# Gated attention mix on one core: each product of weights and values split over the two halves of the array's rows

## The chip, the cores and the metric

The kernel runs on one core of one Trainium2 chip. Its engines are TensorE (PE in the profile, with PEld for its weight loads), VectorE (DVE), ScalarE (ACT), GpSimd (POOL) and SyncE (SP, which here issues DMAs). TensorE writes its results to PSUM, which has eight banks of 128 partitions by 512 fp32 numbers. The metric is the device time of one execution in microseconds (us), median of several runs.

## The reference

Two attention blocks, A and B, work on the same input x, with weights of their own. Both have 32 heads of 20 features, 2048 tokens and a model width of 640. A gate per token mixes their outputs.

```python
def _A_ref(x, wqkv, wo):                 # _B_ref is the same
    B, S, D = x.shape                    # 1, 2048, 640
    H = 32; Dh = D // H                  # 32 heads of 20
    qkv = (x @ wqkv).reshape(B, S, 3, H, Dh).transpose(2, 0, 3, 1, 4)
    q, k, v = qkv[0], qkv[1], qkv[2]
    p = softmax(einsum("bhqd,bhkd->bhqk", q, k) * Dh ** -0.5, axis=-1)
    o = einsum("bhqk,bhkd->bhqd", p, v)
    return o.transpose(0, 2, 1, 3).reshape(B, S, D) @ wo

g = sigmoid((x * gate_w).sum(-1, keepdims=True))
return g * _A_ref(x, A_wqkv, A_wo) + (1 - g) * _B_ref(x, B_wqkv, B_wo)
```

## The kernel before

**Units and steps.** The 64 heads of A and B are taken in 16 groups of four (GH = 4), and the 2048 queries in four blocks of 512 (QB). One group with one block of queries is a unit; there are 64. A unit's 2048 keys are taken in eight steps of two tiles of 128 keys. So the main loop, over G, has 16 x 4 x 8 = 512 steps.

**What a step does on TensorE.**
- *Scores* (`scores`, L644): for each of the two key tiles and four heads one product with 64 rows, keys against queries, 128 x 512, in a bank of its own. Even heads lie in rows 0 to 63 of the array, odd ones in rows 64 to 127. ScalarE takes the exponential from the bank into an SBUF tile `pt` of 128 keys by 512 queries, fp32 (L647).
- *Maxima* (`max_mm`, L581): the softmax needs each query's largest score before its exponentials are made. It is found up to 15 steps ahead, by products of 60 rows, queries against 512 keys, one in either half of the rows. VectorE reduces most of these banks (L592). Where two chunks of keys are taken together, ScalarE makes a ReLU of a difference (L585), and VectorE combines it with the other bank (L589).
- *Values* (`values`, L662): for each key tile of the step before, one block of four products, one for each head: the stationary operand is 128 keys by 21 columns of V (20 features and a column of ones, which gives the softmax's sum), fp32; the moving operand is `pt`. The four heads write the partitions 0, 32, 64 and 96 on of one bank, `acc`, and are summed there over all 16 key tiles of the unit.
- *Blocks of other work* (L382): projections of later groups (q, k and v from x, as products of fp16 halves) and output projections, up to 15 full-width products into one bank, one block at place 3 of a step's eight places (and at place 6 when it is behind). They are emptied by L409, L537, L727 and L729. Small products are L605, L768, L167 and L184.

**Order.** Everything is issued in an order written out in the loop at the end of the kernel. The eight places q of a step each have one score product and one or two products for maxima; the two blocks of values stand at places 0 and 5 (VPOS), other blocks at places 3 and 6. Each engine takes its instructions in that order.

**Banks.** Seven of the eight banks rotate (`banks`, NB = 7); the eighth is `acc`. `take` chooses, while the program is made, the bank that a small planner expects to be free first. The planner keeps a clock for TensorE, ScalarE and VectorE with estimated costs (`tick_score`, `tick_block`, `spend`, `give`); at run time only the semaphores decide, and a product waits until its own bank was emptied.

**End of a unit.** After the unit's last values, `take_acc` copies `acc` to the SBUF tile `ot` on ScalarE (L747), and the next unit's first values, which overwrite the bank, wait for that copy. The rest is spread over later steps: the sums are inverted, multiplied in (L770) and split into fp16 halves on GpSimd, and SyncE stores them. `take_last` (L788) does this for the last unit without a detour.

**Start.** x is transposed by TensorE (`turn`, L859) into rotating banks; the first six transposed blocks are kept in banks until the scale of x is known, and are then drained by ScalarE and VectorE (L863, L864).

Of the kernel before, what the change touches and what calls it, by code (L numbers as in the profile page):

```python
# [11 lines left out]
F32 = mybir.dt.float32  # L12
I32 = mybir.dt.int32
AF = mybir.ActivationFunctionType
OP = mybir.AluOpType
# [4 lines left out]
P = 128  # L20
# [4 lines left out]
NT = S // P  # L25
NC = D // P
GH = 4
NG = H // GH
GF = GH * DH
QB = 512  # L30
# [4 lines left out]
VW = DH + 1  # L35
# [9 lines left out]
RAMP = 1.5  # L45
BETWEEN = 1.3
VSTART = 14
NB = 7

T_SCORE, T_MODE, T_VALUES, T_READY = 0.217, 0.1, 0.85, 0.39  # L50
T_EXP, T_MAX, T_BACK = 0.478, 0.6, 0.15
# [8 lines left out]
def kernel(  # L60
# [10 lines left out]
    nc = tc.nc  # L71
# [7 lines left out]
    psum = ctx.enter_context(tc.tile_pool(name="psum", bufs=1, space=PSUM))  # L79
# [18 lines left out]
    V = [consts.tile([P, NT, 2 * GH, VW], F32, name=f"v{i}") for i in range(2)]  # L98
    sums = consts.tile([P, P], F32, name="sums")
    nc.gpsimd.tensor_copy(sums.rearrange("p (h e) -> p h e", e=32),  # L100
                          ident.rearrange("p (h e) -> p h e", e=32)[:, :, DH:VW].to_broadcast([P, GH, 32]))
    acc = psum.tile([P, QB], F32, name="acc")
    banks = [psum.tile([P, QB], F32, name=f"bank{i}") for i in range(NB)]
    gates = consts.tile([P, 2, NT], F32, name="gates")
    inv_x = consts.tile([P, 1], F32, name="inv_x")
# [14 lines left out]
    block_end = [0.0, None]  # L120
    free_at, held = [0.0] * NB, set()
    now = [-1]

    def take():

        i = min((k for k in range(NB) if k not in held), key=lambda k: free_at[k])
        held.add(i)
        return i, banks[i]

    def spend(engine, cost, ready=0.0):  # L130

        clock[engine] = max(clock[engine], ready) + cost
        return clock[engine] + T_BACK

    def give(i, t):
        free_at[i] = t
        held.discard(i)
# [7 lines left out]
    def tick_block(cost, ready=0.0):  # L145

        begin = block_end[0] if now[0] < 0 and block_end[1] == rows_free else max(rows_free) + T_MODE
        clock["pe"] = max(begin, ready)
        rows_free[:] = [clock["pe"] + cost + T_MODE] * 2
        block_end[:] = [clock["pe"] + cost, list(rows_free)]  # L150
        clock["done"] = clock["pe"] + cost + T_READY - T_MODE
# [60 lines left out]
    def scales_qk(i, maxima):  # L212

        return scales(maxima, 2, lambda r, inv: set_qk(i, r, inv))
# [171 lines left out]
    def turns(n):  # L386

        for _ in range(n if now[0] >= 0 else 0):
            yield
# [30 lines left out]
    def run(gen):  # L420
        for _ in gen:
            pass
# [35 lines left out]
    def half_tiles(g):  # L458
        blk["q", g] = wts.tile([P, 2, 1024], F16, name="cq", tag="cq", bufs=2)
        return blk["q", g]  # L460
# [93 lines left out]
    def unit_of(u):  # L554
        gq, i = divmod(u, NS)
        g, qb = divmod(gq, NQ)
        return g, qb, i
# [3 lines left out]
    def max_parts(g, qb):  # L561
        m = mparts[g, qb] = wts.tile([P, 2, 2, 4, 4], F32, name="mpart", tag="mpart", bufs=2)
        nc.gpsimd.memset(m[:, :, 0:1 if g else 2, :, 0] if g or qb else m, LOW)
# [62 lines left out]
    ptiles, weighed = {}, {}  # L626
# [30 lines left out]
    def values(G, kk):  # L657
        g, qb, i = unit_of(G)
        tick_block(T_VALUES, weighed.pop((G, kk)))
        kt = 2 * i + kk  # L660
        for h in range(GH):
            nc.tensor.matmul(acc[32 * h:32 * h + VW, :], V[(g // 2) % 2][:, kt, (g % 2) * GH + h, :],  # L662
                             ptiles.pop((G, kk, h)), start=(kt == 0), stop=(kt == NT - 1))


    wo_parts = {}
# [76 lines left out]

    def take_acc(g, qb):

        ot = work.tile([P, QB], F32, name="ot", bufs=2)
        nc.scalar.activation(ot, acc, AF.Copy)  # L747
        spend("act", T_EXP)
        few, many = (2, 8) if g == 2 * NG - 1 else (6, 24)
        sq = work.tile([P, 16], F32, name="sq", bufs=2)  # L750
        sh = work.tile([P, 2, 16], F16, name="sh", bufs=2)
        yield from turns(few)
        nc.sync.dma_start(sq, ot.rearrange("(h e) q -> h e q", e=32)[:, DH, :])
        yield from turns(many)
        nc.vector.reciprocal(sq, sq)
        spend("dve", 0.25)
        nc.gpsimd.tensor_scalar(sq, sq, RS, None, op0=OP.mult)
        nc.gpsimd.tensor_copy(sh[:, 0], sq)
        nc.gpsimd.tensor_tensor(sh[:, 1], sq, sh[:, 0], op=OP.subtract)
        yield from turns(few)  # L760
        sr = work.tile([2 * GH, QB], F16, name="sr", bufs=1)
        for k in range(2):
            nc.sync.dma_start(sr[GH * k:GH * k + GH], sh[:, k])
        yield from turns(many)
        yield PRODUCT
        i, pt = take()
        tick_block(T_SCORE, free_at[i])
        nc.tensor.matmul(pt, sel.rearrange("k h e -> k (h e)"), sr, start=True, stop=True)  # L768
        yield
        nc.vector.tensor_tensor(ot, ot, pt, op=OP.mult)  # L770
        give(i, spend("dve", 0.7, clock["done"]))
        o = work.tile([P, 2, QB], F16, name="on", bufs=2)
        nc.gpsimd.tensor_copy(o[:, 0], ot)  # L773
        nc.gpsimd.tensor_tensor(o[:, 1], ot, o[:, 0], op=OP.subtract)
        if g < 2 * NG - 1:
            yield from turns(16)
            for h in range(GH):
                f = (g % NG * GH + h) * DH
                nc.sync.dma_start(o_scr[g // NG][:, f:f + DH, qb * QB:(qb + 1) * QB].rearrange("k d q -> d k q"),
                                  o[32 * h:32 * h + DH])  # L780
            stored.add((g, qb))
        else:
            last.append((qb, o))

    def take_last():

        ot = work.tile([P, QB], F32, name="ot", bufs=2)
        nc.scalar.activation(ot, acc, AF.Copy)  # L788
        i, pt = take()
        nc.tensor.matmul(pt, sums, ot, start=True, stop=True)  # L790
        rc = work.tile([P, QB], F32, name="fs")
        o = work.tile([P, 2, QB], F16, name="on", bufs=2)
        for t in range(4):
            c = slice(t * P, (t + 1) * P)
            nc.vector.reciprocal(rc[:, c], pt[:, c])
            nc.vector.tensor_tensor(ot[:, c], ot[:, c], rc[:, c], op=OP.mult)
            nc.scalar.activation(o[:, 0, c], ot[:, c], AF.Copy)
            nc.gpsimd.tensor_tensor(o[:, 1, c], ot[:, c], o[:, 0, c], op=OP.subtract)
        give(i, spend("dve", 4.0, spend("act", T_EXP)))
        return o  # L800
# [19 lines left out]
            nc.sync.dma_start(out_t[:, 4 * qb + t, :], y)  # L820


    nc.vector.memset(acc, 0.0)
    start_stack = ExitStack()
    start = start_stack.enter_context(tc.tile_pool(name="start", bufs=1))
    xs = start.tile([P, NT, D], F32, name="xs")
# [26 lines left out]
    def turn(j0, c):  # L853

        n = slice(j0 * P, (j0 + 4) * P)
        i, pt = take()
        for u in range(4):
            tick_block(0.11, free_at[i])
            nc.tensor.transpose(pt[:, u * P:(u + 1) * P], xs[:, j0 + u, c * P:(c + 1) * P], ident)  # L859

        def drain():
            give(i, spend("dve", T_MAX, spend("act", T_EXP, clock["done"])))
            nc.scalar.activation(xh[:, c, n], pt, AF.Copy, scale=r_x)  # L863
            nc.vector.scalar_tensor_tensor(xl[:, c, n], pt, r_x, xh[:, c, n], op0=OP.mult, op1=OP.subtract)  # L864

        return drain

    def turns_of(j0, cs=range(NC)):
        for c in cs:
            turn(j0, c)()  # L870
            yield

    max_parts(0, 0)
    drains = [turn(0, c) for c in range(NC)] + [turn(4, 0)]
    found = []
    run(scales(wm, 5, lambda r, inv: found.extend((r, inv))))
    r, inv = found
# [4 lines left out]
    for f in drains:  # L882
# [7 lines left out]
                            op=OP.subtract)  # L890
# [4 lines left out]
    def a_chunk(ch):  # L895
        if ch % 2 == 0:
            halves.append(half_tiles(0))
        n = slice((ch % 2) * QB, (ch % 2 + 1) * QB)
        hl = halves[ch // 2][:, :, n]
        yield from project_chunk(blk["a", 0], hl[:, 0], hl[:, 1], ch)  # L900
        for pair in range(2):
            run(spread(0, hl, ch * QB, QB, q=(0,) if ch == pair == 0 else (), k=(pair,), queues=both))
# [7 lines left out]
    def beside(gen, n, other):  # L910

        for k, _ in enumerate(gen):
            if k % n == n - 1:
                next(other, None)
        run(other)
# [6 lines left out]
        key_differences(0, halves[half], start.tile([P, QB], F32, name="fd"), start.tile([P, 2, QB], F16, name="dd0"))  # L922
        run(spread_differences(0, both, to))

    beside(a_chunk(0), 2, turns_of(4, range(1, NC)))
    beside(a_chunk(1), 3, turns_of(8))
    differences_of(0, KD[0])
    beside(a_chunk(2), 3, turns_of(12))
# [29 lines left out]
    work = ctx.enter_context(tc.tile_pool(name="work", bufs=2))  # L958
# [22 lines left out]
    for g in range(2 * NG):  # L981
        b = g * NQ * NS
        n = g + 1
        if n < 2 * NG:
# [3 lines left out]
            i = g // 4 + 1  # L988
            if i < 4:
                if g % 4 == 0:  # L990
                    z, c0 = i // 2, 320 * (i % 2)
                    parts = max_tasks([[(wqkv[z], part * D + c0 + 160 * k) for k in range(2)] for part in range(2)],
                                      lambda m, i=i: scales_qk(i, m))
# [98 lines left out]
    for G in range(STEPS + 1):  # L1092
        g, qb, i = unit_of(G)
# [8 lines left out]
        for q in range(8):  # L1102
# [22 lines left out]
            if q == 3:  # L1125
                for f in todo.pop(G, []):
                    f()
                out_tasks(G)
    end_o = take_last()
    while side or parked or fill or current or outs or last:  # L1130
        advance()
# [32 lines left out]
```

## Time and profile before

| | |
|---|---|
| median of three runs | 2894.9 us (2893.07 to 2895.11) |
| the profiled execution's own time | 2894.15 us |
| its span, first to last instruction | 2892.3 us |
| mean granted TensorE clock | 0.995 of full speed |
| TensorE busy (PE) | 2816.3 us, 97% |
| ScalarE busy (ACT) | 2552.8 us, 88% |
| VectorE busy (DVE) | 2431.3 us, 84% |
| GpSimd busy (POOL) | 672.8 us, 23% |

A row of the timeline has the start in us from the span's begin, the duration, engine, line, operation, output and inputs, their shapes, and how many records were merged; in brackets stands how long the engine was idle before it, and what ended that. For a product, `128*21` is the rows and columns of the array that it uses. A row of the groups has the busy time, the mean duration of one in ns, and the idle time before with what ended it. A row of the windows has the stretch, its length, and then for PE, PEld, DVE, ACT and POOL the busy us with the number of instructions, followed by the granted clock, the DMA share and GB/s. A record of a product covers its way through the array too, so records of products that follow each other overlap, and the distance between starts tells more than the duration. An fp32 product is two records.

### The profile page before, as it was taken

The numbers are of one execution on the slowest core, as the hardware profiler recorded it, in microseconds if no ns is written. First come the engines' busy times: TensorE is split into PE (matmuls) and PEld (weight loads), VectorE is DVE, ScalarE is ACT, GpSimd is POOL, SyncE is SP. The second block draws the span as 40 slices with busy tenths as digits, with TensorE's granted clock in tenths as the row PEclk, the third lists the DMA queues.
The fourth block names the chain that finished last, engine by engine and source line by source line (L and its number), as shares of the span: only waits on it lengthen the run. The fifth ranks groups of instructions, "written<-read, shape, count | busy, mean of one in ns | idle before, by whom it ended". The sixth has DMA issues, their size and how long they took to land.

```text
span 2892.3 us, 63590 instructions
## 1 busy us (share of the span) xinstructions
PE 2816.3 (97%) x23474; PEld 979.8 (34%) x23474; DVE 2431.3 (84%) x4643; ACT 2552.8 (88%) x5249; POOL 672.8 (23%) x1096
## 2 busy tenths in 40 slices
PE   6899999999999999999999999999999999999998
PEld 3433223342233323343233333334333333332222
DVE  6688898878898898978988888887788888889973
ACT  3799999989999999988989999998899999888986
POOL 5212112121221212233331111212113243120010
PEclk9999999999999999999999999999999999999999
DMA  4110101001020101102022020111102112122122
GB/s 128 36 45 7 36 11 40 16 12 33 13 53 17 31 15 28 46 13 52 17 47 50 13 59 16 44 39 24 44 21 52 44 39 69 52 67 72 54 61 71
DMA packets 176765, 114.80 MB, mean 40 GB/s; under 512 B 111812, under 2 KB 150396, under 8 KB 176452
## 3 DMA queue, kind: packets, MB, share of 16 engines
q1 hardware_dynamic: 174196, 109.77, 15.8%
q8 instruction: 184, 3.01, 0.4%
q0 software_dynamic: 1600, 0.96, 0.2%
q14 instruction: 129, 1.06, 0.1%
q10 hardware_dynamic: 656, 0.00, 0.0%
HBM read 48.89 MB, written 26.61 MB: 26 GB/s over the span
## 4 chain that ended last, share of the span: by engine, by line
PE 90%; DVE 4%; ACT 2%; DMA 1%; POOL 1%; issue 1%; SPq 0%; DVEq 0%; ACTq 0%; POOLq 0%
PE acc L662 33%; PE bank L644 23%; PE bank L382 19%; PE bank L581 12%; DVE mpart L592 3%; ACT pt L647 2%; PE bank L768 1%; DMA xs<-in_A_x_dram 0%; PE bank L605 0%; PE bank L815 0%; ACT rl L585 0%; DVE mneg L599 0%; DMA wv<-in_A_wqkv_dram 0%; PE bank L184 0%; PE bank L859 0%
## 5 line engine op out<-in xcount | busy, mean ns | idle before, releaser
L647 ACT ACTIVATE pt<-bank 128x512 f32<-128x512 f32 x4096 | 2223.0, 612 | 222.8 <-PE bank L581 194.3
L592 DVE TENSOR_REDUCE mpart<-bank 128x1 f32<-128x512 f32 x2976 | 1912.2, 684 | 342.0 <-PE bank L581 271.1
L644 PE MATMUL bank<-qt,kt 64*128 64x512 f16 x4096 | 1164.8, 381 | 11.6 <-ACT pt L647 7.2
L662 PE MATMUL acc<-pt,v 128*21 128x512 f32 x8192 | 1081.9, 600 | 0.5
L581 PE MATMUL bank<-kt,qt 60*128 60x512 f16 x3536 | 1050.3, 380 | 4.7 <-ACT pt L647 0.7
L644 PEld LDWEIGHTS <-kt 64*128 64x128 f16 x4096 | 281.0, 94 | 1092.7 <-issue 914.6
L589 DVE CUSTOM_DVE_ANT_0 rl<-bank,rl 128x512 f32<-128x512 f32 x560 | 378.6, 681 | 16.2 <-PE bank L581 7.0
L585 ACT ACTIVATE rl<-bank 128x512 f32<-128x512 f32 x560 | 329.4, 594 | 7.9 <-PE bank L581 7.9
L581 PEld LDWEIGHTS <-qt 60*128 60x128 f16 x4096 | 270.8, 94 | 67.3 <-issue 53.9
L382 PE MATMUL bank<-xx,wbh 128*128 128x168 f16 (+2 forms) x2240 | 283.3, 244 | 9.8 <-ACT pt L647 4.3
L662 PEld LDWEIGHTS acc<-pt,v 128*21 128x21 f32 x8192 | 142.9, 99 | 399.1 <-issue 361.7
L773 POOL CAST on<-ot 128x512 f16<-128x512 f32 x63 | 38.5, 611 | 928.4 <-DVE ot L770 891.8
L382 PE MATMUL bank<-xx,wbl 128*128 128x168 f16 (+2 forms) x1120 | 253.4, 243 | 0.0
L382 PEld LDWEIGHTS <-wbh 128*128 128x128 f16 x2240 | 184.5, 98 | 99.9 <-issue 89.8
L581 PE MATMUL bank<-kd,qt 60*128 60x512 f16 x560 | 208.1, 387 | 1.8 <-DMA kd<-dd 1.2
L382 PE MATMUL bank<-woh,o_in 128*128 128x160 f16 (+1 forms) x960 | 156.7, 256 | 4.8 <-ACT pt L647 2.8
L382 PE MATMUL bank<-wvh,xx 128*128 128x160 f16 (+1 forms) x1280 | 155.4, 233 | 5.9 <-ACT pt L647 3.7
L382 PEld LDWEIGHTS <-xx 128*128 128x128 f16 x1920 | 133.5, 97 | 57.8 <-issue 52.5
L382 PE MATMUL bank<-wvl,xx 128*128 128x160 f16 (+1 forms) x640 | 137.3, 231 | 0.6 <-POOL wvl L322 0.6
L382 PEld LDWEIGHTS <-o_in 128*128 128x128 f16 (+1 forms) x1440 | 105.6, 97 | 73.9 <-issue 60.4
L411 POOL CAST cq<-fs 128x512 f16<-128x512 f32 x60 | 36.7, 611 | 364.8 <-ACT fs L409 364.8
L382 PE MATMUL bank<-wol,o_in 128*128 128x160 f16 (+1 forms) x480 | 115.7, 254 | 0.0
(132 smaller groups left out, 1347.3 us busy)
## 6 DMA issues: line engine op xcount, KB each, us to landing
y_scr<-y_out SPq DMA_DIRECT2D x32, 320.0 KB
kt<-cq SPq DMA_DIRECT2D x120, 80.0 KB
o_scr<-on SPq DMA_DIRECT2D x240, 40.0 KB
kt<-cq SPq DMA_DIRECT2D x136, 40.0 KB
xs<-in_A_x_dram SPq DMA_DIRECT2D x8, 640.0 KB
o_in<-o_scr SPq DMA_DIRECT2D x32, 160.0 KB
y_out<-y_scr SPq DMA_DIRECT2D x16, 320.0 KB
xx<-y_scr SPq DMA_DIRECT2D x16, 320.0 KB
```

The lines of the kernel that those rows point to most:

```text
L382: nc.tensor.matmul(out_ap, a, b, start=(k == 0), stop=(k == len(pairs) - 1))
L411: nc.gpsimd.tensor_copy(hi, f)
L581: nc.tensor.matmul(pt, QT[g % 2][r, pair, q0:q0 + P], k, start=True, stop=True)
L585: nc.scalar.activation(relus[u, j], pt, AF.Relu)
L589: nc.vector.tensor_tensor_reduce(rl, pt, rl, 1.0, LOW, OP.add, OP.max, m)
L592: nc.vector.tensor_reduce(m, pt, axis=AX.X, op=OP.max)
L644: nc.tensor.matmul(et, KT[g % 2][r, pair, kt * P:(kt + 1) * P], QT[g % 2][r, pair, qb * QB:(qb + 1) * QB], start=True, stop=True)
L647: nc.scalar.activation(pt, et, AF.Exp, scale=factor(g // 4))
L662: nc.tensor.matmul(acc[32 * h:32 * h + VW, :], V[(g // 2) % 2][:, kt, (g % 2) * GH + h, :], ptiles.pop((G, kk, h)), start=(kt == 0), stop= ...
L768: nc.tensor.matmul(pt, sel.rearrange("k h e -> k (h e)"), sr, start=True, stop=True)
L773: nc.gpsimd.tensor_copy(o[:, 0], ot)
```

## The change

Each product of a head's weights and values over 128 keys becomes two over 64 keys: keys 0 to 63 in rows 0 to 63 of the array, keys 64 to 127 in rows 64 to 127. The two halves are summed in a bank each, `acc0` and `acc1`. At the end of a unit (`sum_acc`), ScalarE copies the first bank to `ot` as before, and VectorE adds the second bank to it. With two banks for sums, six are left to rotate (NB = 6). At the start, five transposed blocks are held in banks ahead of the scales, and the sixth moves behind them to the others of its row of tiles.

```diff
-NB = 7
+NB = 6
...
-    acc = psum.tile([P, QB], F32, name="acc")
+    acc = [psum.tile([P, QB], F32, name=f"acc{i}") for i in range(2)]
...
         for h in range(GH):
-            nc.tensor.matmul(acc[32 * h:32 * h + VW, :], V[(g // 2) % 2][:, kt, (g % 2) * GH + h, :],
-                             ptiles.pop((G, kk, h)), start=(kt == 0), stop=(kt == NT - 1))
+            pt = ptiles.pop((G, kk, h))
+            for half in range(2):
+                r = slice(64 * half, 64 * half + 64)
+                nc.tensor.matmul(acc[half][32 * h:32 * h + VW, :], V[(g // 2) % 2][r, kt, (g % 2) * GH + h, :], pt[r],
+                                 start=(kt == 0), stop=(kt == NT - 1))
+
+    def sum_acc():
+
+        ot = work.tile([P, QB], F32, name="ot", bufs=2)
+        nc.scalar.activation(ot, acc[0], AF.Copy)
+        spend("act", T_EXP)
+        nc.vector.tensor_tensor(ot, ot, acc[1], op=OP.add)
+        spend("dve", T_MAX)
+        return ot
...
     def take_acc(g, qb):
 
-        ot = work.tile([P, QB], F32, name="ot", bufs=2)
-        nc.scalar.activation(ot, acc, AF.Copy)
-        spend("act", T_EXP)
+        ot = sum_acc()
...
     def take_last():
 
-        ot = work.tile([P, QB], F32, name="ot", bufs=2)
-        nc.scalar.activation(ot, acc, AF.Copy)
+        ot = sum_acc()
...
-    nc.vector.memset(acc, 0.0)
+    for t in acc:
+        nc.vector.memset(t, 0.0)
...
-    drains = [turn(0, c) for c in range(NC)] + [turn(4, 0)]
+    drains = [turn(0, c) for c in range(NC)]
...
-    beside(a_chunk(0), 2, turns_of(4, range(1, NC)))
+    beside(a_chunk(0), 2, turns_of(4))
```

## The prediction

> **What bounds the kernel now.** I read the page from the top: the engines' shares, the clock, then the chain that ended last.
>
> ```profile
> span 2892.3 us, 63590 instructions
> PE 2816.3 (97%) x23474; PEld 979.8 (34%) x23474; DVE 2431.3 (84%) x4643; ACT 2552.8 (88%) x5249; POOL 672.8 (23%) x1096
> PEclk9999999999999999999999999999999999999999
> PE acc L662 33%; PE bank L644 23%; PE bank L382 19%; PE bank L581 12%; DVE mpart L592 3%; ACT pt L647 2%; PE bank L768 1%; DMA xs<-in_A_x_dram 0%; PE bank L605 0%; PE bank L815 0%; ACT rl L585 0%; DVE mneg L599 0%; DMA wv<-in_A_wqkv_dram 0%; PE bank L184 0%; PE bank L859 0%
> ```
>
> TensorE is the bound at full clock, and the line that the change rewrites, L662, is a third of the chain. But ScalarE and VectorE, which empty the banks, are not far behind. Since an average hides stages, I next took a stretch from the middle:
>
> ```profile
> 1500.00:2000.00 500.00, 495.87 (x4418) 183.30 (x4417) 422.67 (x801) 451.13 (x937) 103.70 (x177) 1.00 0.16 36
> ```
>
> Columns: PE, PEld, DVE, ACT, POOL. PE 99%, ACT 90%, DVE 85%: three engines almost in balance, joined by seven banks. A program that takes a bank away has to be read for its waits, not only for PE's work. So the last view is the timeline of PE over part of one step:
>
> ```profile
> 1509.10 0.59 PE L644 MATMUL bank<-qt,kt 64*128 64x512 f16 x2
> 1509.32 0.38 PE L581 MATMUL bank<-kt,qt 60*128 60x512 f16 x1
> 1509.62 1.06 PE L662 MATMUL acc<-pt,v 128*21 128x512 f32 x8
> 1510.61 0.39 PE L644 MATMUL bank<-qt,kt 64*128 64x512 f16 x1
> 1510.62 0.39 PE L581 MATMUL bank<-kd,qt 60*128 60x512 f16 x1
> 1510.84 0.38 PE L581 MATMUL bank<-kt,qt 60*128 60x512 f16 x1
> 1510.84 0.59 PE L644 MATMUL bank<-qt,kt 64*128 64x512 f16 x2
> 1511.06 0.38 PE L581 MATMUL bank<-kt,qt 60*128 60x512 f16 x1
> 1511.37 0.24 PE L382 MATMUL bank<-woh,o_in 128*128 128x160 f16 x1
> ```
>
> The pattern: six score and maximum products in pairs, one in each half of the rows, a pair every 0.22 us (1510.62, 1510.84, 1511.06); a block of values (L662); six more; a projection block (L382). A last pair started at 1509.32 streams until 1509.54, and values start at 1509.62: a gap of 0.08. They take 0.99 us to the next score at 1510.61.
>
> **Values, part by part.** A block is four products, each as two passes (eight records). Cutting the timeline inside the block shows its first four passes alone:
>
> ```profile
> 1509.62 0.63 PE L662 MATMUL acc<-pt,v 128*21 128x512 f32 x4
> L662 PE MATMUL acc<-pt,v 128*21 128x512 f32 x8192 | 1081.9, 600 | 0.5
> ```
>
> Four records of about 0.60 end within 0.63, so they start some 0.007 us apart and run side by side in four column groups; the second four start 1.06 - 0.63 = 0.43 to 0.44 us later. 8192 records of eight are 1024 blocks. Of 0.99, two passes are 0.88, the stagger 0.02, and 0.09 is left before the score.
>
> After the change a block is sixteen passes on eight tiles, 64 rows by 32 columns. The halves hold disjoint rows and write different banks, as the pairs of scores already do, so I let all eight run together. The array time stays two passes; the stagger grows by four starts: 4 x 0.007 = 0.027, x 1024 = **+28 us**. Bounds: 0 if each second half starts with its first, as in a score pair (1510.61 and 1510.62), and +911 us if the halves run after each other (two more passes, 0.89 x 1024; a rival below). I take 28, since its row is of this very product.
>
> The Trainium skill prices packed tiles at about 4 ns for each further tile (TensorE: Matmul & The Clock Gate, Part 3, "Measured speedup vs the span model"). By that, an estimate, four more tiles cost 16 ns a block and 17 us in all; the 7 ns above is measured here and decides.
>
> **The gaps at the mode switch** are what a split into halves could save: scores use 64 rows, values 128. If that difference alone drains the array, both gaps of about 0.09 would go. These rows speak on it:
>
> ```profile
> 600.43 0.28 PE L605 MATMUL bank<-ident,mneg 128*16 128x128 f32 x1
> 600.63 1.05 PE L662 MATMUL acc<-pt,v 128*21 128x512 f32 x8
> 89.43 0.31 PE L382 MATMUL bank<-wvh,xx 128*128 128x161 f16 x2
> 89.57 0.27 PE L605 MATMUL bank<-ident,mneg 128*16 128x128 f32 x1
> 89.68 0.23 PE L382 MATMUL bank<-wvl,xx 128*128 128x161 f16 x1
> 2871.50 0.30 PE L815 MATMUL bank<-wbl,on 128*128 128x320 f16 x1
> 2871.63 0.30 PE L815 MATMUL bank<-wbh,on 128*128 128x320 f16 x1
> 2871.86 1.06 PE L662 MATMUL acc<-pt,v 128*21 128x512 f32 x8
> ```
>
> The transpose L605 fits between two full-width products with no gap (0.11 to the next start), so it runs in their mode: 128 rows, full columns. From it to values, only the columns change, and they start 0.20 after it, 0.09 more. L815's products follow each other after 0.13, and values follow L815 after 0.23, again 0.10 more. A change of columns alone costs the same gap. Scores use 128 columns and the new values 32, so I keep both gaps: **0 us**, bounds -184 us (0.18 x 1024) and 0.
>
> Eight more weight loads and eight more products a block must also be issued. The densest stretch:
>
> ```profile
> 86.50:91.50 5.00, 5.00 (x72) 4.97 (x71) 1.68 (x7) 2.91 (x11) 1.29 (x4) 1.00 0.00 0
> ```
>
> 143 instructions in 5 us, 35 ns each. The stretch 1500 to 2000 has 4418 + 4417 = 8835 PE instructions. The program has 512 steps, so some 512/2892 x 500 = 89 in this stretch, with two blocks of values each and 16 more instructions a block: 8835 + 89 x 32 = 11,680, or 43 ns each. Above 35: issue hides behind the streams, **0**.
>
> **Six banks instead of seven.** This is the costly part. Beside the group at 1510.61 stand
>
> ```profile
> 1510.26 0.60 ACT L647 ACTIVATE pt<-bank 128x512 f32<-128x512 f32 x1
> 1511.10 0.60 ACT L647 ACTIVATE pt<-bank 128x512 f32<-128x512 f32 x1 [0.24 <-PE bank L581]
> 1509.93 2.65 DVE L592 TENSOR_REDUCE mpart<-bank 128x1 f32<-128x512 f32 x4
> ```
>
> When the group starts at 1510.61, ScalarE holds one bank until 1510.86, and VectorE, whose four reductions end every 0.66 (1510.6, 1511.2, 1511.9, 1512.6), holds the one that ends at 1511.2. The group takes six: 2 + 6 - 1 = 7 at 1511.06. With six banks the last product waits for 1511.2. Then the L382 block, which began at 1511.37, needs a bank too, and the next to come free is that of the exponential of 1511.10, at 1511.70: 0.33 late, and a signal more, so 0.35. That the delay isn't made up later I read from ScalarE's 0.24 of waiting for PE: its backlog is used up within each step, so it moves along. With 4 products ahead of a block of values nothing waits, and values take no bank. How many such blocks there are is told by what empties them:
>
> ```profile
> L409 ACT ACTIVATE fs<-bank 128x168 f32<-128x168 f32 (+1 forms) x216 | 72.8, 337 | 24.2 <-PE bank L382 23.7 <-POOL on L773 0.5
> L537 ACT ACTIVATE v<-bank 128x160 f32<-128x160 f32 x128 | 42.5, 332 | 6.2 <-PE bank L382 5.6
> L727 ACT ACTIVATE y_out<-bank,f_o 128x160 f32<-128x160 f32 x64 | 26.7, 417 | 1.7 <-PE bank L382 1.6
> L729 DVE SCALAR_TENSOR_TENSOR y_out<-bank,f_o,y_out 128x320 f32<-128x320 f32 x32 | 17.6, 551 | 8.8 <-PE bank L382 5.4 <-ACT pt L647 3.0
> L729 DVE SCALAR_TENSOR_TENSOR xx<-bank,f_o,xx 128x320 f32<-128x320 f32 x32 | 17.5, 550 | 28.9 <-PE bank L382 27.4 <-PE bank L581 0.7 <-PE bank L644 0.6
> ```
>
> 216 + 128 + 64 + 32 + 32 = 472 blocks x 0.35 = **+165 us**. Bounds: 0 if the consumers' slack (10% of ACT) takes it up, and (472 + 512) x 0.35 = +344 if one group before values in each of the 512 steps waits as long.
>
> **Taking the sums.** At the end of a unit the accumulator is copied, and now the second is added on VectorE:
>
> ```profile
> 976.52 0.38 PE L581 MATMUL bank<-kt,qt 60*128 60x512 f16 x1
> 976.86 1.06 PE L662 MATMUL acc<-pt,v 128*21 128x512 f32 x8
> 976.21 0.60 ACT L747 ACTIVATE ot<-acc 128x512 f32<-128x512 f32 x1 [0.19 <-PE acc L662]
> 976.53 0.69 DVE L592 TENSOR_REDUCE mpart<-bank 128x1 f32<-128x512 f32 x1
> L770 DVE TENSOR_TENSOR ot<-ot,bank 128x512 f32<-128x512 f32 x63 | 43.0, 682 | 0.0
> ```
>
> The copy ends at 976.81, and the next values, which overwrite the accumulator, start at 976.86, where the last score pair lets them anyway. The add has the form of L770, 0.68, starts after the copy at 976.87 and ends at 977.55; only then may values begin, on all of PE's queue, 0.7 to 0.75 late. The add stands in VectorE's queue ahead of the reduction of 976.53, so that one and its bank are late too, but PE stands still meanwhile. 63 x 0.75 = **+47 us**; bounds 0 (if values were held by banks there anyway) and 63 x 1.44 = 91 (VectorE has one more reduction of 0.69 ahead). The last unit's add and the four transposes that move behind the scales add **+1**. The add's 43 us of VectorE work lie in its 16% of idle time. The second memset lies beside the loads.
>
> **Sum.** Against the profiled execution's own time, 2894.15 (0.75 below the median of 2894.9, so no correction): 28 + 0 + 165 + 47 + 1 = 241, which is 3135. I forecast **3130 us**, since a few of the stops fall together.
>
> **Rivals.**
> (1) *The bank waits are absorbed.* For: ACT and DVE idle 10 and 15%. Against: ScalarE already waits for PE in the step shown. 2894 + 28 + 48 = 2970.
> (2) *Twice the bank waits*, at values as well: 2894 + 28 + 344 + 48 = 3314. For: seven banks are all in use at 1511.06; against: in the group at 1509.10 six suffice.
> (3) *The halves don't run together*, so the change doesn't do what it says: + 911 + 47; bank waits vanish behind the longer blocks: 3850. Against: scores' halves do, and column groups do; no row shows both at once.
> (4) *Faster*: the row mode is what drains, and both gaps at values vanish: 2894 - 184 + 28 + 48 = 2786 with no bank wait. It decides only while a block's wait is under (184 - 76)/472 = 0.23 us; at 0.35 the time is 2951, slower still. For: no row shows 64 rows going from 128 to 32 columns. Against: L605 and L815 above.
>
> The Trainium skill stands against (4): a change of tiling mode, not of tile, drains the array (TensorEngine Tiling (Array Packing), "Key Properties"). By that rule (4) has no gain left and ends at 3135 or 2970.
>
> **Chances.** Forecast 57%; (1) 18%; (2) 6%; (3) 8%; (4) with its gaps gone 11%, of which 6% on the faster side and 5% near 2951. About 0.2% is what a measurement can tell from no change. Faster 0.06, same 0.02 (the edge of (4)), slower 0.92. The range takes in the forecast, (1) and the slower half of (4), and leaves out (3), the fast half of (4) and the top of (2): 2945 to 3270.
>
> **What would show it.** In L662's rows: sixteen passes within about 1.09 us; two starts at +0.43, not at +0.9. The gap to the next score still 0.09. PE's idle time before L382 and L581, now small, shows ScalarE and VectorE as releasers with some 165 us, and the shares of ACT and DVE fall to about 82 and 79%. Before the first values of a unit, PE waits about 0.7 for the add. I am wrong if L662's block is shorter than now, if PE shows no more bank waits, or if block time doubles.

## The result and the profile after

The changed kernel takes 3134.16 us (median of four runs, 3130.92 to 3135.13), against 2893.99 for the kernel before on the same chips: a ratio of 1.0829 (95% interval 1.0812 to 1.0846), **240 us slower**. 3130 was forecast.

First the page of the changed kernel: its span, the engines, the chain; then the window 1500 to 2000, and two rows of the groups (L665 is the line of the values now).

```profile
span 3133.3 us, 79158 instructions
PE 2980.5 (95%) x31666; PEld 1032.1 (33%) x31666; DVE 2486.8 (79%) x4708; ACT 2602.3 (83%) x5249; POOL 672.0 (21%) x1096
PE acc L665 30%; PE bank L382 18%; PE bank L644 18%; PE bank L581 11%; ACT pt L647 10%; DVE mpart L592 4%; ACT ot L671 1%; PE bank L778 1%; DMA xs<-in_A_x_dram 0%; PE bank L605 0%; DVE mneg L599 0%; PE bank L824 0%; ACT rl L585 0%; DMA wv<-in_A_wqkv_dram 0%; PE bank L184 0%
1500.00:2000.00 500.00, 482.41 (x5293) 166.72 (x5285) 408.58 (x767) 430.35 (x873) 102.95 (x170) 1.00 0.14 32
L665 PE MATMUL acc<-pt,v 64*21 64x512 f32 x16384 | 1107.2, 597 | 0.0
L581 PE MATMUL bank<-kt,qt 60*128 60x512 f16 x3536 | 1121.7, 379 | 62.9 <-ACT pt L647 52.7 <-DVE mpart L592 1.5
```

ScalarE and VectorE fall to 83 and 79% (forecast: 82 and 79), and the exponential L647 rises from 2% to 10% of the chain: PE now waits for what empties its banks. But the idle time of PE in front of L581 is only 63 us. The rest of the wait doesn't look idle: PE's busy time grew by 164 us (2816.3 to 2980.5), though its own work hardly grew. A record of a score lasts 0.38 us, and the next pair is due 0.22 after it, so a start that comes up to 0.16 late leaves no idle time between the records. So starts have to be read. The timeline of PE over one stretch that answers to the one shown of before, with the first passes of its block cut out (second row), and then ScalarE and VectorE beside it:

```profile
1641.06 1.08 PE L665 MATMUL acc<-pt,v 64*21 64x512 f32 x16
1641.06 0.65 PE L665 MATMUL acc<-pt,v 64*21 64x512 f32 x8
1642.08 0.39 PE L644 MATMUL bank<-qt,kt 64*128 64x512 f16 x1
1642.08 0.39 PE L581 MATMUL bank<-kd,qt 60*128 60x512 f16 x1
1642.30 0.38 PE L581 MATMUL bank<-kt,qt 60*128 60x512 f16 x1
1642.31 0.59 PE L644 MATMUL bank<-qt,kt 64*128 64x512 f16 x2
1642.71 0.37 PE L581 MATMUL bank<-kt,qt 60*128 60x512 f16 x1
1643.15 0.23 PE L382 MATMUL bank<-woh,o_in 128*128 128x160 f16 x1
```
```profile
1641.37 1.28 DVE L592 TENSOR_REDUCE mpart<-bank 128x1 f32<-128x512 f32 x2
1642.50 0.60 ACT L647 ACTIVATE pt<-bank 128x512 f32<-128x512 f32 x1 [0.19 <-PE bank L581]
1642.99 0.59 ACT L585 ACTIVATE rl<-bank 128x512 f32<-128x512 f32 x1
```

The block of values is sixteen passes of 0.60: eight start within 0.05 (0.65 - 0.60), the others 0.43 to 0.44 later, and the next score starts 1.02 after the first, 0.03 more than before. The halves do run together. Then five products go as ever, but the sixth, which would start at 1642.52 beside the second of the two L644, waits until 1642.71 for the reduction that gives its bank back (the second of two, over at 1641.37 + 1.28 = 1642.65). The projection block waits for the exponential of 1642.50, which ends at 1643.10, and starts at 1643.15. From the first of the six to the block it is 1.07 us; in the rows of before it was 0.76 (1510.61 to 1511.37).

This can be summed over the whole trace. A stretch is the time from the first score or maximum product after a stop to the next stop (values, block or small product), by the starts of products; sums in us. One block of the trace after, whose next score itself came 0.86 late, is counted in the last row.

| stretch (count) | before | after |
|---|---|---|
| values, first pass to next score (1022 before, 1021 after) | 1011.3 | 1034.3 |
| six products, then a block (389) | 324.8 | 449.5 |
| six products, then values (430) | 332.1 | 376.5 |
| ten products, then values or a small product (95) | 185.0 | 224.4 |
| all else of the span | 1039.1 | 1048.6 |

Of some 240 us, 23 lie in the values themselves, 125 ahead of blocks, 44 ahead of values, 39 in steps without a block, and 10 elsewhere. The 44 lie at one place: the 55 stretches ahead of a unit's first values take 90.0 us against 45.3, and the other 375 take 286.5 against 286.9.

### The profile page after: what moved, and what is told of

Same layout as the page of the kernel before. It is cut to its first block, busy times and chain, and to the rows that moved or that the text cites. A ratio compares the mean times of both kernels' runs of the same rounds, so it can differ in the third digit from the quotient of the medians.

```text
span 3133.3 us, 79158 instructions
## 1 busy us (share of the span) xinstructions
PE 2980.5 (95%) x31666; PEld 1032.1 (33%) x31666; DVE 2486.8 (79%) x4708; ACT 2602.3 (83%) x5249; POOL 672.0 (21%) x1096
## 4 chain that ended last, share of the span: by engine, by line
PE 80%; ACT 11%; DVE 4%; issue 2%; DMA 1%; POOL 1%; SPq 0%; DVEq 0%; ACTq 0%; POOLq 0%
PE acc L665 30%; PE bank L382 18%; PE bank L644 18%; PE bank L581 11%; ACT pt L647 10%; DVE mpart L592 4%; ACT ot L671 1%; PE bank L778 1%; DMA xs<-in_A_x_dram 0%; PE bank L605 0%; DVE mneg L599 0%; PE bank L824 0%; ACT rl L585 0%; DMA wv<-in_A_wqkv_dram 0%; PE bank L184 0%
## 5 line engine op out<-in xcount | busy, mean ns | idle before, releaser
L647 ACT ACTIVATE pt<-bank 128x512 f32<-128x512 f32 x4096 | 2221.0, 603 | 381.6 <-PE bank L581 354.5
L644 PE MATMUL bank<-qt,kt 64*128 64x512 f16 x4096 | 1176.5, 381 | 13.8 <-ACT pt L647 5.7
L581 PE MATMUL bank<-kt,qt 60*128 60x512 f16 x3536 | 1121.7, 379 | 62.9 <-ACT pt L647 52.7
L665 PE MATMUL acc<-pt,v 64*21 64x512 f32 x16384 | 1107.2, 597 | 0.0
L644 PEld LDWEIGHTS <-kt 64*128 64x128 f16 x4096 | 280.7, 94 | 1115.8 <-issue 947.5
L665 PEld LDWEIGHTS acc<-pt,v 64*21 64x21 f32 x16384 | 166.6, 95 | 462.2 <-issue 451.7
L581 PEld LDWEIGHTS <-qt 60*128 60x128 f16 x4096 | 270.0, 94 | 60.0 <-issue 50.7
L581 PE MATMUL bank<-kd,qt 60*128 60x512 f16 x560 | 208.6, 387 | 2.2 <-DMA kd<-dd 1.2
L613 POOL CAST m4r<-mt 16x128 f16<-16x128 f32 x128 | 33.0, 282 | 421.6 <-ACT mt L610 421.6
```

The source lines that it names most:

```text
L581: nc.tensor.matmul(pt, QT[g % 2][r, pair, q0:q0 + P], k, start=True, stop=True)
L613: nc.gpsimd.tensor_copy(m4[:, k, :], mt)
L644: nc.tensor.matmul(et, KT[g % 2][r, pair, kt * P:(kt + 1) * P], QT[g % 2][r, pair, qb * QB:(qb + 1) * QB], start=True, stop=True)
L647: nc.scalar.activation(pt, et, AF.Exp, scale=factor(g // 4))
L665: nc.tensor.matmul(acc[half][32 * h:32 * h + VW, :], V[(g // 2) % 2][r, kt, (g % 2) * GH + h, :], pt[r], start=(kt == 0), stop=(kt == NT - 1))
```

## The experiments

Theory: the bank that the second accumulator takes makes most of the loss, the split itself little. Rivals: the split products cost PE more than their stagger, or the add at a unit's end holds PE. Times are medians; each ratio is to the kernel before on the same chip.

**Six banks alone.** The kernel before, with

```diff
-NB = 7
+NB = 6
...
-    drains = [turn(0, c) for c in range(NC)] + [turn(4, 0)]
+    drains = [turn(0, c) for c in range(NC)]
...
-    beside(a_chunk(0), 2, turns_of(4, range(1, NC)))
+    beside(a_chunk(0), 2, turns_of(4))
```

> The kernel before with six rotating banks and nothing else changed: one accumulator, whole products of 128 keys, no add. Theory (the missing bank alone makes most of the loss, at the stretch of six score and maximum products ahead of a projection block): 2894 + about 170 = 3065 us, 3045 to 3085, and that stretch 0.31 us longer in the median, as in the changed kernel. Rival (the split products fill the array or the queue, and PE waits because of them): at most 20 us above before, under 2915. The part of the split alone would then be the rest to 3134 less the add: about 25 us by the first, over 150 us by the second.

3092.64 us, ratio 1.0685 (1.0667 to 1.0703): +199 without any split. The first rival is out. The theory holds in kind but not in size: 199, not 170, although the stretch before blocks (437.1) is no longer than in the changed kernel. The surprise is the stretch of six products before values: 375.1, as long as in the changed kernel (376.5), though this kernel has no add.

**The changed kernel without the add.**

```diff
         nc.scalar.activation(ot, acc[0], AF.Copy)
         spend("act", T_EXP)
-        nc.vector.tensor_tensor(ot, ot, acc[1], op=OP.add)
-        spend("dve", T_MAX)
         return ot
```

> The changed kernel without the add of the second accumulator at the end of a unit, so the sums of keys 64 to 127 are left out of the output. Theory (the next values wait for the copy and then for the add): 63 units x 0.70 to 0.75 us less, 3087 to 3095 us, and no stretch of six products before values over 0.9 us. Rival (values are held by banks at that place anyway, so the add hides): within 10 us of 3134.

3116.21 us, ratio 1.0768 (1.075 to 1.0786): 18 us less than with the add, between both expectations. Against the run with six banks, the split alone is 3116 - 3093 = 24 us. And the stretches before values stay at 376.0. The timeline of a unit's end shows why, first in the changed kernel, then without the add:

```profile
1142.53 0.39 PE L644 MATMUL bank<-qt,kt 64*128 64x512 f16 x1
1142.74 0.60 ACT L671 ACTIVATE ot<-acc 128x512 f32<-128x512 f32 x1 [0.40 <-issue]
1143.37 0.69 DVE L673 TENSOR_TENSOR ot<-ot,acc 128x512 f32<-128x512 f32 x1 [0.65 <-PE bank L644]
1143.88 0.37 PE L581 MATMUL bank<-kt,qt 60*128 60x512 f16 x1 [0.53 <-ACT pt L647]
1144.18 0.65 PE L665 MATMUL acc<-pt,v 64*21 64x512 f32 x8
```
```profile
1137.10 0.39 PE L644 MATMUL bank<-qt,kt 64*128 64x512 f16 x1
1137.31 0.60 ACT L671 ACTIVATE ot<-acc 128x512 f32<-128x512 f32 x1 [0.40 <-issue]
1138.44 0.37 PE L581 MATMUL bank<-kt,qt 60*128 60x512 f16 x1 [0.53 <-ACT pt L647]
1138.75 0.65 PE L665 MATMUL acc<-pt,v 64*21 64x512 f32 x8
```

Both take 1.65 from the first score to the values; six products ahead of other values take 0.76. In both, the sixth product waits for an exponential. It stands in ScalarE's queue behind the copy, and ScalarE stood idle for 0.40 ahead of the copy. The add ends at 1144.06, before the sixth product's record ends at 1144.25, and so hides under a wait that is there without it.

**Two copies in place of the add.**

```diff
-        nc.vector.tensor_tensor(ot, ot, acc[1], op=OP.add)
+        o2 = work.tile([P, QB], F32, name="fs")
+        nc.vector.tensor_copy(o2, acc[1])
         spend("dve", T_MAX)
+        nc.gpsimd.tensor_tensor(ot, ot, o2, op=OP.add)
```

> The changed kernel with another way to sum the two accumulators: VectorE copies the second bank to a tile of its own without waiting for ScalarE's copy of the first, and GpSimd adds the two tiles. Both banks are then free about 0.65 us after the last values. Theory A (as predicted: the next values wait for copy and add one after the other, 0.75 us in each of 63 units): 3134 - 40 = about 3095 us. Theory B (formed on the run without the add: the next values are held by a bank at that place anyway, and the add costs only 18 us, because VectorE waits for the copy and is late for the next block's banks): 3115 to 3128 us, and the stretch of six products before a unit's first values stays near 1.6 us.

3134.17 us, ratio 1.0833 (1.0818 to 1.0847): nothing gained, so both theories miss. What the add costs is not its own wait. The copy has VectorE's time too:

```profile
L674 DVE COPY fs<-acc 128x512 f32<-128x512 f32 x64 | 43.8, 684 | 1.0 <-PE acc L665 0.9
```

and the stretches before blocks are 448.4, as with the add (449.5) and not as without (436.1). The next run agrees.

**Six banks, the copy on VectorE.**

```diff
-        nc.scalar.activation(ot, acc, AF.Copy)
-        spend("act", T_EXP)
+        nc.vector.tensor_copy(ot, acc)
+        spend("dve", T_MAX)
```

> The kernel before with six rotating banks (3092.6 us), with the copy of the accumulator at a unit's end on VectorE and not on ScalarE. Theory (with six banks the sixth product before a unit's first values waits for an exponential that stands in ScalarE's queue behind the copy): the 43 us at these stretches go or shrink to under 20, 3055 to 3075 us. Rival (any engine that copies is as late with a bank): 3085 to 3100 us.

3092.61 us, ratio 1.0688 (1.0674 to 1.0703): the rival's value. The stretches before values shrink (362.0 from 375.1), and those before blocks grow as much (449.6 from 437.1). At a unit's end:

```profile
1127.18 0.69 DVE L747 COPY ot<-acc 128x512 f32<-128x512 f32 x1
1127.40 0.60 ACT L647 ACTIVATE pt<-bank 128x512 f32<-128x512 f32 x1 [0.58 <-PE bank L581]
1128.05 0.37 PE L581 MATMUL bank<-kt,qt 60*128 60x512 f16 x1 [0.25 <-ACT pt L647]
1128.35 0.63 PE L662 MATMUL acc<-pt,v 128*21 128x512 f32 x4
```

The copy is over at 1127.87, long before the values; the sixth product still waits for an exponential, though ScalarE was idle ahead of it. The three kernels with 0.68 us of VectorE's time more at a unit's end have 448 to 450 us before blocks; without it the four with blocks at the same place have 436 to 438 (the two below among them). Between the kernels with and without the add, all of this difference lies in 49 stretches, those ahead of the first block after a unit's first values (69.5 against 56.9 us).

**Two accumulators in turn.** Six banks, whole products, and unit by unit the other of two accumulators; then the same with the copy two places of the step later.

```diff
-    acc = psum.tile([P, QB], F32, name="acc")
+    acc = [psum.tile([P, QB], F32, name=f"acc{i}") for i in range(2)]
...
-            nc.tensor.matmul(acc[32 * h:32 * h + VW, :], V[(g // 2) % 2][:, kt, (g % 2) * GH + h, :],
+            nc.tensor.matmul(acc[G // NS % 2][32 * h:32 * h + VW, :], V[(g // 2) % 2][:, kt, (g % 2) * GH + h, :],
...
+        yield from turns(3)          # only in the second of the two kernels
         ot = work.tile([P, QB], F32, name="ot", bufs=2)
-        nc.scalar.activation(ot, acc, AF.Copy)
+        nc.scalar.activation(ot, acc[(g * NQ + qb) % 2], AF.Copy)
```

> Six rotating banks and whole products (3092.6 us), with the eighth bank used as a second accumulator that units take in turn, so the next unit's values never wait for the copy, which stays where it stands in ScalarE's queue. It tells apart what holds PE at a unit's end. Theory C (ScalarE waits in its queue for the last values, copies, and its exponentials come late, so the sixth product waits for a bank): no gain, 3080 to 3095 us, the stretch before a unit's first values stays near 1.6 us. Theory D (the values wait for the copy): the stretch falls to 0.8 us, 3050 to 3060 us.

> The same with the copy two places of the step later in ScalarE's queue, behind two more exponentials. Theory C: ScalarE no longer waits for the values, the bank of the sixth product comes in time, and most of the 43 us at the units' ends goes: 3050 to 3070 us. Theory D: the same time as with the copy in its old place, within 5 us.

3091.97 us (ratio 1.0684, 1.067 to 1.0699) and 3080.69 us (1.0644, 1.063 to 1.0659). Freeing the values of the copy gives nothing (374.9 us before values), moving the copy 11 us (361.7). So theory D is out: with six banks, values don't wait for the copy. C has the direction, but not the size: of the 43 us at the units' ends, some 13 go. The rest isn't the copy's time on ScalarE, as a unit's end of the second kernel shows:

```profile
1122.12 0.68 DVE L771 TENSOR_TENSOR ot<-ot,bank 128x512 f32<-128x512 f32 x1
1122.59 0.39 PE L644 MATMUL bank<-qt,kt 64*128 64x512 f16 x1
1123.01 0.60 ACT L647 ACTIVATE pt<-bank 128x512 f32<-128x512 f32 x1 [0.58 <-PE bank L581]
1123.66 0.37 PE L581 MATMUL bank<-kt,qt 60*128 60x512 f16 x1 [0.25 <-ACT pt L647]
1123.98 0.60 ACT L748 ACTIVATE ot<-acc 128x512 f32<-128x512 f32 x1
```

The copy (L748) comes after the wait, and the exponential that ends it is that of the first of the same six products (1122.59), for which ScalarE stood waiting. Meanwhile a bank is empty: the one that the multiplication L771 read until 1122.80. In the program, `take` has given the sixth product the bank of the first, and leaves the empty one to the next six. With six banks that is so at all 55 units' ends, in the changed kernel too. The planner books the multiplication with `clock["done"]`, which by then is the end of the block of values, and so expects its bank 0.02 us after the other; in the traces it is free 0.2 to 0.8 after the first score, and the other only after 1.0 to 1.3. So most of the 43 us come from this choice among six banks, not from a bank that is missing there. No run gives the sixth product the empty bank.

Ahead of blocks this is rare without the add: in the run with six banks alone, a bank had stood empty for 0.15 or more in 6 of the 304 late starts of a sixth product. With the add, it is so in 40 of the 49 stretches that grew. The planner books the add's time too, so whether VectorE's time or the choice makes those 13 us wasn't separated.

**Five banks.** The kernel before with `NB = 5`, and four transposed blocks held at the start (five with six banks).

> The kernel before with five rotating banks; one transposed block fewer is held at the start. Theory (banks are short in runs of six products and more, and each bank that is missing puts off the end of each such run, now also before values): more than the step from seven to six, which cost 199 us; 3092 + 250 to 400 = 3340 to 3490 us. Rival (each bank costs the same): 3290 us; rival (the shortage was that of the seventh bank at blocks alone): under 3200 us.

3495.21 us, ratio 1.2082 (1.2064 to 1.2101). From seven to six banks 199 us, from six to five 403, just beyond the expected range. Now the stretches of six products before values are longer everywhere (608.5 us, from 375.1).

**Blocks one place earlier**, with six banks (the changed kernel) and with seven (the kernel before):

```diff
-BLOCKS = (3, 6)
+BLOCKS = (2, 6)
```

> The changed kernel with projection blocks one place earlier in a step, so that four score and maximum products and not six stand between values and the block, and six between the block and the next values, which need no rotating bank. Theory (six banks are short only where a seventh is wanted at once, by the block behind six products): most of the 125 us at blocks goes, 3000 to 3040 us; the steps without a block, with ten products on end, keep their wait. Rival (six banks are too few in the mean for the way through TensorE, ScalarE and VectorE): the waits only move, 3115 to 3150 us.

> The kernel before, seven banks and whole products, with blocks one place earlier as in the run with six banks. Theory (there the stretch of six products before a block loses only 30 us in all over its shortest length): 2865 to 2895 us. Rival (six products ahead of values leave less to VectorE and ScalarE during the longer stop): slower, 2900 to 2930 us.

With six banks 3086.65 us, ratio 1.0667 (1.0649 to 1.0684): 47 us gained and not 125, between the two expected ranges. With seven 2872.67 us, ratio 0.9929 (0.9912 to 0.9945), **21 us faster than the kernel before**. The wait before blocks is gone in both (four products and a block: 0.548 and 0.540 us in the mean). But with six banks much of it comes back at the other stops: of the stretches with six products ahead of values there are 701 now (638.5 us against 543.7 with seven banks), and 115 have a small product (L605, L768 and the like) at their end, which wants a seventh bank too (134.1 against 91.1). With six banks, theory and rival are each half right; with seven, the theory's range was met.

**Even runs.** Seven banks, blocks at place 2, and in steps without a block the second values at place 4:

```diff
+        vpos = list(VPOS)
...
-                if q == VPOS[k]:
+                if q == vpos[k]:
...
-            if q == BLOCKS[0] or (q == BLOCKS[1] and behind(G)):
+            if q == BLOCKS[0]:
+                if not slot(G):      # slot now says whether there was one
+                    vpos[1] = 4
+            elif q == BLOCKS[1] and behind(G):
                 slot(G)
```

> Seven banks, whole products, blocks one place earlier (2872.7 us in the earlier run), and in steps that have no block the second values one place earlier as well, so that ten and six products become eight and eight. Theory (in those steps, too, banks are short because the run is long; its 73 + 22 runs of ten take 1.9 us where five pairs and a gap would take 1.2): 2825 to 2850 us. Rival (in a step without a block ScalarE and VectorE have more to do than PE, and PE waits for them however the products lie): 2865 to 2880 us.

2891.38 us, ratio 0.9994 (0.9985 to 1.0003): the gain of the earlier blocks is lost, slower than both expected. The runs of eight take 1.47 us before values, where four pairs and a gap would take 0.97; splitting the run evenly just puts a wait in both halves. It fits that the emptying engines set the pace in these steps, but that wasn't shown by itself.

## Why the prediction was right, and where it wasn't

The time was met within 4 us, and the main cause, that one bank fewer rotates, is shown by the run with six banks. That the time came so close is luck: two of its terms were off by about 30 us each, one up and one down, and cancelled.

- **The stagger**: +28 forecast, 23 in the stretches, 24 by the difference of two runs. Eight first passes within 0.05 make 0.007 a start. The Trainium skill's 4 ns a tile (TensorE: Matmul & The Clock Gate, Part 3, "Measured speedup vs the span model") is too low here: 16 us by it, an estimate (16 ns x 1024; the prediction's 17 is a slip).
- **The gaps at the mode switch**: 0 forecast, and so it is. In the rows after, the sixth product of 1642.71 streams 0.22, and the block follows late for its bank; but at the unit's end shown, the product of 1138.44 streams until 1138.66 and values of 64 rows start at 1138.75: 0.09 as ever, with 64 rows on both sides. Rival (4) had its gain there and is out. The Trainium skill's rule that a change of tiling mode drains (TensorEngine Tiling (Array Packing), "Key Properties") agrees.
- **Issue**: 0 forecast. Passes still start 0.007 apart, so nothing came late from the queue.
- **Six banks**: +165 forecast, 199 measured by the run with nothing else changed. That the block behind six products waits was right, and its price nearly: 0.35 forecast, (437.1 - 324.8) / 389 = 0.29 measured there, 0.32 with the add. The count was wrong: 472 blocks, where only 389 come behind six products. So blocks make 112 of the 199 us, and most of the rest lies at two places that the sum put at nothing: runs of ten products (39 us) and the units' ends (43 us), where the working took for granted that a product gets whatever bank is free. The upper bound of 344 was far off, since six products ahead of all other values do fit.
- **Taking the sums**: +47 forecast, from the step "only then may values begin, on all of PE's queue, 0.7 to 0.75 late". This step failed. Values begin 44 us later at these places, but so they do without an add: they wait behind the sixth product, which was given a bank that an exponential holds. The add itself is worth 18 us, 13 of them ahead of the next block. The lower bound, "if values were held by banks there anyway", was the truth at that place.
- **Rivals**: by (1), waits absorbed, the run with six banks would have come near 2894, by (2), twice the waits, near 2894 + 344 = 3238; it took 3093. (3), halves one after the other, is out by the row with x8.
- **What would show it**: PE's idle time was to show some 165 us with ScalarE and VectorE as releasers. It shows 63 in front of L581. The place to look is the distance between starts.

## What to carry to other kernels

Before giving a bank away, mark in the timeline how many banks are in use at each stop of TensorE; if the last is taken just ahead of a stop that wants one more, price each such stop by when the next bank comes free, and count stops by what stands ahead of them, not by their number in all. Where the program fixes which bank a product takes, look also at which one it was given: with fewer banks a wrong guess costs a wait although another bank is empty. A wait that you take away or add may lie under another at the same place: run the suspected cause alone. And where three engines are nearly in balance, moving a stop so that fewer products stand ahead of it can gain more (here 0.7%) than changing the work.

## What was not expected of the hardware

A record's busy time hides waits: PE was busy 164 us longer for 23 us of added work. And one thing was forecast that no row of before showed: sixteen fp32 passes on eight tiles of 64 rows by 32 columns run in the array time of eight on four. Their block is 1.02 us to the next score, the old one 0.99.
